# Recall of the fourth chunk placed in the first two steps of the feed-forward loop, with later feature splits and fewer, larger feature loads

## The chip, the core and the metric

The program runs on one core of a Trainium2 chip. A core has five engines with queues of their own: TensorE (PE) multiplies matrices into PSUM, VectorE (DVE), ScalarE (ACT) and GpSimd (POOL) work on vectors, and SyncE (SP) issues the transfers between memory and SBUF; sixteen DMA engines carry them. Each engine works through its own instructions in the order in which they stand; where an instruction waits on another engine, all that stands behind it on its queue waits too. The metric is the device time of one execution in microseconds (us), the median of some runs.

## The reference

`x` has 2048 tokens of 576 features. The result mixes an attention branch and a gated feed-forward branch by a gate that is computed for each token. The attention branch has 32 heads of 18 features and goes through the tokens in four chunks of 512; beside the attention inside a chunk, each chunk reads a memory that was summed over the chunks before it.

```python
scale = Dh ** -0.5
mask = (ar[:, None] < ar[None, :]) * (-1e9)
g = _sigmoid(beta).reshape(1, H, 1, 1)
for s in range(N):
    qs, ks, vs = q[:, :, s], k[:, :, s], v[:, :, s]
    p = _softmax(einsum("bhqd,bhkd->bhqk", qs, ks) * scale + mask)
    a_dot = einsum("bhqk,bhkd->bhqd", p, vs)
    pq = phi(qs)                                   # t + 1 where t > 0, else exp(t)
    num = einsum("bhld,bhde->bhle", pq, M)
    den = einsum("bhld,bhd->bhl", pq, z)[..., None] + 1e-6
    outs.append(g * num / den + (1.0 - g) * a_dot)
    pk = phi(ks)
    M = M + einsum("bhld,bhle->bhde", pk, vs)
    z = z + einsum("bhld->bhd", pk)
...
b = (_gelu(x @ w_gate) * (x @ w_up)) @ w_down
out = gate * (a @ wo) + (1 - gate) * b
```

## The kernel before

All large products are made from pairs of 16-bit words (a high and a low part), which ACT and POOL or DVE split off the 32-bit values. The program has two parts that matter here, and a last one (the output products) that doesn't.

**The projections** (lines 874 to 1171) go through the four chunks `s = 0..3` (the text counts them as chunks 1 to 4). In each, PE first makes the rows of `v` (`vrows`, eight products in four quarters `q`), and then nine products `j = 0..8` of 14 matmuls each (`project`, line 414), which give the columns of `q` and `k`. One product later `put_columns` takes such a product out of PSUM: ACT writes its high words (line 684) and, where features are needed, `relu` and `exp` (689, 690); DVE makes the positive part (697) and the low words (703); POOL adds the two into the feature tile `phi` (698). PSUM banks go round by name: `j = 0` has `dn`, 3 and 7 have `U`, 4 and 8 have `G`, the others `st` (two of them).

**The features of `q`** (`j` up to 4) of chunks 2 to 4 are needed with the features in rows. `split_phi` (658) makes words of each tile as soon as the next `put_columns` runs (ACT line 663, POOL line 664) and stores them to memory (`phq`, lines 666 and 667). `load_phi` (669) reads them back, a group of eight heads at a time: four pairs of heads, in two tiles of two pairs (three such tiles exist), by eight loads of 64 rows. `recall(s, g)` (751) multiplies a group by the memory (`mpair`), 16 small matmuls; `put_recall` (763) divides on DVE (771 to 775) and stores the result `mo` (two buffers) to `oms` (778). The recalls of chunks 2 and 3 stand in the quarters of the next chunk's rows; those of chunk 4 behind its products 6, 7 and 8 and behind the last `put_columns`.

**The memory.** `key_rows` and `memorize` sum the memory in PSUM, `keep_memory` (811, at `j = 1`) takes it out on DVE, and `memory_pairs` (826, at `j = 2`) squares it on ACT (829), sums the squares on PE (96), scales it on POOL, makes words of it and sends it through memory into `mpair` (851).

**Beside the products** `next_x` (945) squares the next chunk's input on ACT (159), sums the squares on POOL (166), lets PE sum over the rows (178), and makes words of the input with ACT (201) and DVE (218, 223). In chunk 4 the first weights of the feed-forward part are prepared instead: high words on ACT (343, 354), low words on POOL (347, 355), sums of blocks on POOL (332 to 337, `sums_g`).

**The feed-forward loop** (1855) runs 72 steps of `step(v)` (1497). A step is a fixed row of products (line 535, six matmuls of 128x512 each, and 1372) on the banks `G`, `V` and `U`, with DVE copies between them (1548, 1600, 1602, 1638), `gelu` on ACT (1367) and the split of the hidden words on ACT (1356) and POOL (1364). From step 4 on the attention inside the chunks is worked off beside it. Its tiles lie in the pools `keep` and `atn`, which are opened where the pool `prj` of the projections is closed.

The order of PE, ACT, DVE and POOL is that in which the code is written. The order of the transfers on SP isn't written by hand: a scheduler puts them there. Eight transfers can be under way before the next one waits for the oldest.

## Time and profile before

| | |
|---|---|
| time, median of 3 runs | 1616.96 us (1616.36 to 1617.0) |
| time of the profiled execution | 1616.14 us |
| its span, first to last instruction | 1614.1 us |
| PE busy | 1557.5 us |
| ACT, DVE, POOL busy | 1217.8, 1262.4, 1164.0 us |
| granted PE clock, mean | 0.986 |

The span is what the views of the profile cover; it is 2.0 us shorter than the time of its execution. In the views a row of the timeline gives the start, the duration, the line and the operation, with `xN` where N instructions in a row are merged, and in brackets the idle time of the engine ahead of it and what ended it. A row of the windows gives the busy time of each engine in a stretch, the granted clock of PE, the share of the DMA engines and what they moved. The rows themselves stand in the prediction.

### The profile page before, as it was taken

The page shows a single profiled execution, that of the slowest core. Times are in us where ns is not written, and L with a number is a line of the kernel's source. Part 1 is how long each engine was busy: PE and PEld are TensorE (multiplying, and loading weights), DVE is VectorE, ACT ScalarE, POOL GpSimd, SP SyncE. Part 2 cuts the span into 40 slices and gives each one's busy share as a digit, 9 for nine tenths or more (in the row PEclk, how much of TensorE's full clock was granted, in tenths as well). Part 3 has the DMA queues.
Part 4 walks back from the last instruction along what each step waited for, and adds up shares of the span by engine and source line. Part 5 has one row for each costly group of instructions (what it writes and reads, how often), then busy time and mean ns, then how long its engine had stood idle before and what let it go on. Part 6 is the DMA issues. An engine that isn't in the chain of part 4 may idle for free.

```text
span 1614.1 us, 34082 instructions
## 1 busy us (share of the span) xinstructions
PE 1557.5 (96%) x12271; PEld 944.9 (59%) x12271; DVE 1262.4 (78%) x3245; ACT 1217.8 (75%) x2092; POOL 1164.0 (72%) x1264
## 2 busy tenths in 40 slices
PE   9987867999999999999999999999999999999999
PEld 5644533456565665566565665666565665566577
DVE  7756764687888888888888888888888888888665
ACT  7565562487888888887889888888888888887421
POOL 5274481767778786867778786867878786867597
PEclk9999987999999999999999999999999999999999
DMA  6655665056575656666566767666575767755546
GB/s 242 224 154 177 207 179 151 31 102 131 121 141 118 145 139 143 139 132 133 121 145 116 154 129 154 143 131 136 118 151 117 154 137 148 138 122 105 111 84 174
DMA packets 514309, 225.85 MB, mean 140 GB/s; under 512 B 436920, under 2 KB 492956, under 8 KB 513628
## 3 DMA queue, kind: packets, MB, share of 16 engines
q1 hardware_dynamic: 514140, 223.68, 60.7%
q8 instruction: 96, 1.57, 0.4%
q14 instruction: 73, 0.60, 0.1%
HBM read 97.47 MB, written 37.52 MB: 84 GB/s over the span
## 4 chain that ended last, share of the span: by engine, by line
PE 82%; POOL 6%; ACT 3%; DVE 3%; DMA 3%; SPq 2%; issue 2%; POOLq 0%; ACTq 0%; DVEq 0%
PE dn L1326 25%; PE U L535 17%; PE G L535 11%; PE V L535 6%; PE V L1446 5%; PE pv L1279 4%; PE U L1372 2%; SPq L677 1%; PE V L1377 1%; PE G L1377 1%; PE st L1241 1%; PE V L1372 1%; PE G L1372 1%; POOL phi L698 1%; PE dn L421 1%
## 5 line engine op out<-in xcount | busy, mean ns | idle before, releaser
L535 PEld LDWEIGHTS <-pairg 128*128 128x128 f16 x2592 | 248.2, 98 | 262.5 <-issue 17.1
L1262 POOL TENSOR_TENSOR pl<-pb,ph 128x896 f16<-128x896 f32 (+1 forms) x128 | 185.3, 1469 | 210.5 <-ACT ph L1261 210.5
L1326 PE MATMUL dn<-paird,hhr 128*128 128x288 f16 x2115 | 328.7, 286 | 0.1
L1260 ACT ACTIVATE pb<-pb,mb,esc 128x512 f32<-128x512 f32 (+3 forms) x512 | 304.9, 642 | 5.5 <-POOL pl L1262 0.4
L1334 DVE SCALAR_TENSOR_TENSOR acc<-dn,ev,acc 128x288 f32<-128x288 f32 x533 | 262.6, 513 | 39.0 <-PE dn L1326 33.0
L1326 PEld LDWEIGHTS <-hhr 128*128 128x128 f16 x2160 | 207.0, 98 | 78.6 <-issue 11.8
L535 PE MATMUL G<-x,pairg 128*128 128x512 f16 x864 | 211.2, 381 | 2.6 <-DVE stage L703 2.4
L535 PE MATMUL U<-xt,pairg 128*128 128x512 f16 x864 | 210.3, 379 | 0.0
L1326 PE MATMUL dn<-paird,hhd 128*128 128x288 f16 x1275 | 209.9, 286 | 0.0
L1262 POOL TENSOR_TENSOR pb<-pb,ph 128x896 f16<-128x896 f32 (+1 forms) x128 | 179.6, 1403 | 33.8 <-ACT ph L1261 27.8
L1261 ACT ACTIVATE ph<-pb 128x896 f16<-128x896 f32 (+1 forms) x256 | 188.6, 737 | 9.7
L347 POOL TENSOR_TENSOR pairg<-raw,pairg 128x384 f16<-128x384 f32 (+2 forms) x144 | 156.6, 1109 | 16.7 <-ACT pairg L343 16.7
L1244 DVE CUSTOM_DVE_ANT_0 pb<-st,mask 128x512 f32<-128x512 f32 (+1 forms) x256 | 157.2, 614 | 0.0
L1326 PEld LDWEIGHTS <-hhd 128*128 128x128 f16 x1296 | 123.9, 98 | 50.5 <-issue 6.5
L1244 DVE CUSTOM_DVE_ANT_0 pb<-dn,mask 128x256 f32<-128x256 f32 (+1 forms) x192 | 67.2, 375 | 64.1 <-PE dn L1241 62.4
L1367 ACT ACTIVATE gl<-gl,sc 128x512 f32<-128x512 f32 x110 | 75.8, 715 | 46.7 <-DVE gl L1602 24.2
L535 PE MATMUL V<-x,pairg 128*128 128x512 f16 x426 | 105.0, 383 | 0.9 <-DVE gl L554 0.8
L1446 PE MATMUL V<-xt,nest 128*128 128x256 f16 x714 | 105.5, 272 | 0.2 <-DVE hold L1462 0.2
L535 PE MATMUL U<-x,pairg 128*128 128x512 f16 x432 | 105.0, 379 | 0.0
L414 PEld LDWEIGHTS <-wp 128*128 128x128 f16 x504 | 49.5, 100 | 73.9 <-issue 19.5
L1279 PEld LDWEIGHTS <-pt 128*128 128x128 f16 x2560 | 80.8, 96 | 13.1 <-issue 8.4
L1364 POOL TENSOR_TENSOR hhr<-gl,hhr 128x512 f16<-128x512 f32 x64 | 79.7, 1251 | 10.7 <-ACT hhr L1356 10.6
(377 smaller groups left out, 3229.2 us busy)
## 6 DMA issues: line engine op xcount, KB each, us to landing
qkt<-qk SPq DMA_DIRECT2D x256, 108.0 KB
raw<-in_wgu_dram SPq DMA_DIRECT2D x36, 640.0 KB
rawd<-in_wd_dram SPq DMA_DIRECT2D x36, 288.0 KB
qk<-stage SPq DMA_DIRECT2D x32, 256.0 KB
phg<-phq SPq DMA_DIRECT2D x96, 64.0 KB
qk<-stage SPq DMA_DIRECT2D x40, 128.0 KB
vp<-vstage SPq DMA_DIRECT2D x16, 296.0 KB
vt<-vp SPq DMA_DIRECT2D x16, 296.0 KB
```

What stands on the lines that cost most here:

```text
L347: pool.tensor_tensor(spot(f, *p, 1), raw_g[f][:, p[0] : p[1]], spot(f, *p, 0), OP.subtract)
L535: pe.matmul(o, w[:, i, (a + k) * P : (a + k + 1) * P], x[:, b + k], start=start and k == 0 and i == 0 and b == h, stop=k == 1 and i == 1, ...
L1244: dve.tensor_tensor_reduce(scored(a, qi), out[qi], mask[:, L - (qi + 1) * P :], 1.0, -3e38, OP.add, OP.max, mx[a][:, qi : qi + 1])
L1260: act.activation(r, r, AF.Exp, bias=b[:, qi : qi + 1], scale=esc[:, 0, c : c + 1])
L1261: act.activation(h[:, cols], p, AF.Copy)
L1262: pool.tensor_tensor(low[:, cols], p, h[:, cols], OP.subtract)
L1279: pe.matmul(ov, pr[:, 10 * i + COL[qi] // P + kb], v[:, 4 * e + kb, c0 : c0 + VC], start=kb == 0 and i == 0, stop=kb == qi and i == 1)
L1326: pe.matmul(o[:, :NH], hh[:, a, q * P : (q + 1) * P], w[:, b, n * NH : (n + 1) * NH], start=i == 0, stop=i == 5)
L1334: dve.scalar_tensor_tensor(av, o[:, :NH], ev, av, OP.mult, OP.add)
L1364: pool.tensor_tensor(hh[:, 1], t, hh[:, 0], OP.subtract)
L1367: act.activation(t, o, AF.Gelu_apprx_tanh, scale=scl[f // 2][0][:, 2 + c : 3 + c])
L1446: pe.matmul(o, w[:, (7 * c + i) * P : (7 * c + i + 1) * P], x[d], start=start and n == 0, stop=n == 2, skip_group_check=True)
```

## The change

The recalls of chunk 4 leave the projections: `recall(3, 0)` to `recall(3, 3)` now run inside steps 0 and 1 of the feed-forward loop, two in each, behind the product on `U` (line 1592 of before) and behind `product(Y, f, S4, ...)`. The pool `prj` therefore stays open until step 2, and `keep` and `atn` are opened there. `split_phi` takes a tile only four products after its own (two in chunk 4). `memory_pairs` is cut in two: the squares on ACT at `j = 1`, the rest at `j = 3` instead of 2. A group is loaded by two transfers of four pairs each into one tile of four pairs (two such tiles), and the first load of chunks 2 and 3 moves from `j = 6` to `j = 8`. `mo` has one buffer instead of two. `key_scale` moves from the product at which the next input is scaled into the first quarter of that chunk's rows, and its last operation from POOL to DVE. Every matmul of before is still there.

```diff
-            for i in range(2):
-                t = phg[s, g, i] = pp.tile([P, 2, L], F16, name="phg", bufs=3)
-                for e in range(2):
-                    for k in range(2):
-                        o = (8 * g + 4 * i + 2 * k + e) * n
-                        sp.dma_start(t[64 * e : 64 * e + 64, k], r[o : o + 64])
+            t = phg[s, g] = pp.tile([P, 4, L], F16, name="phg", bufs=2)
+            for e in range(2):
+                o = (8 * g + e) * n
+                sp.dma_start(t[64 * e : 64 * e + 64], r[o : o + 8 * n].rearrange("(k x) t -> x k t", x=2 * n)[:64])
...
-        def split_phi():
-            while phis:
+        def split_phi(until):
+            while phis and phis[0][:2] <= until:
...
-            split_phi()
+            split_phi((s, j - (2 if s == 3 else 4)))
...
-            mo = pp.tile([P, 4, 8 * DH], F32, name="mo", bufs=2)
+            mo = pp.tile([P, 4, 8 * DH], F32, name="mo", bufs=1)
...
-        def memory_pairs(s):
+        def memory_squares():
             q = pp.tile([P, 2], F32, name="msq", bufs=1)
             for i, c in enumerate((slice(0, DH), slice(DH, MC))):
                 act.activation(m16[:, :, 2, c], mc[:, :, c], AF.Square, accum_out=q[:, i : i + 1])
+            return q
+
+        def memory_pairs(s, q):
...
-            pool.tensor_scalar(ali[:, s], al[:, s, 0:3:2], iv, None, OP.mult)
+            dve.tensor_scalar(ali[:, s], al[:, s, 0:3:2], iv, None, OP.mult)
...
-                    key_scale(c)
...
+                        if q == 0:
+                            key_scale(s)
...
-                    if s and j == 2:
-                        memory_pairs(p)
+                    if s and j == 1:
+                        square = memory_squares()
+                    if s and j == 3:
+                        memory_pairs(p, square)
...
-                    if s and j == 6:
+                    if s in (1, 2) and j == 8:
                         load_phi(s, 0)
-                    if s == 3 and j > 5:
-                        recall(3, j - 6, (("V",), ("pv",)) if j == 7 else (("dn", 2), ("dn", 2)))
-                        load_phi(3, j - 5)
             put_columns(*done)
             finish_later()
-            recall(3, 3)
+            load_phi(3, 0)
             ahead[0] = first_product(0)
...
+            if v < 2:
+                recall(3, 2 * v)
+                load_phi(3, 2 * v + 1)
+                finish_later()
             product(X, f, A12, x1, 2, 6)
...
             product(Y, f, S4, x2_, 2, 6)
+            if v < 2:
+                recall(3, 2 * v + 1)
+                if v == 0:
+                    load_phi(3, 2)
+                finish_later()
...
+                if v == 2:
+                    prj.close()
+                    kp = tail.enter_context(tc.tile_pool(name="keep", bufs=2, side="right", reuse_waits="tile"))
+                    home.update(d=kp)
+                    ap_ = atn.enter_context(tc.tile_pool(name="atn", bufs=2, side="right", reuse_waits="tile"))
                 step(v)
```

**SP at the end of chunk 3's products.** `phg` is a group's features on their way back (line 677), `phq` their store, `raw<-in_wgu` the first weights of the feed-forward part, `qk` the words of a product. Before:

```order
L667 DMA phq_67<-stage 64x512
L666 DMA phq_67<-stage 64x1024
L708 DMA qk<-stage 128x2x512
L709 DMA qk<-stage 128x512
L677 DMA phg<-phq_67 64x512 x3
L708 DMA qk<-stage 128x2x512
L709 DMA qk<-stage 128x512
L243 DMA raw<-in_wgu_dram 128x1280 x3
```

Now:

```order
L243 DMA raw<-in_wgu_dram 128x1280
L668 DMA phq_67<-stage 128x1024
L669 DMA phq_67<-stage 128x512
L243 DMA raw<-in_wgu_dram 128x1280 x2
L708 DMA qk<-stage 128x2x512
L709 DMA qk<-stage 128x512
L677 DMA phg<-phq_67 64x4x512 x2
L668 DMA phq_67<-stage 64x1024
```

The first group's loads stood ahead of the three weight loads and now stand behind all of them, and behind the stores of the features of `j = 3`.

**ACT in the first products of chunk 4**, from the taking out of `j = 0`. `m` is the memory's tile of words, `msq` its sums of squares, `hhr`, `pairg` and `xt` words for the feed-forward part. Before:

```order
L690 ACTIVATE expm<-expm,lnv 128x512
L354 ACTIVATE hhr_2643<-raw 128x256
L343 ACTIVATE pairg<-raw 128x384
L343 ACTIVATE pairg<-raw 128x512
L457 ACTIVATE xt_2642<-acc,xsc 128x1024
L684 ACTIVATE stage<-st,unq 128x512
L689 ACTIVATE expm<-st,nal 128x512
L690 ACTIVATE expm<-expm,lnv 128x512
L663 ACTIVATE stage<-phi 128x512
L829 ACTIVATE m_103,msq<-mc 128x5x18
L829 ACTIVATE m_103,msq<-mc 128x5
L840 ACTIVATE m_103<-mt 128x5x19
```

Now:

```order
L690 ACTIVATE expm<-expm,lnv 128x512
L828 ACTIVATE m_103,msq<-mc 128x5x18
L828 ACTIVATE m_103,msq<-mc 128x5
L354 ACTIVATE hhr_2590<-raw 128x256
L343 ACTIVATE pairg<-raw 128x384
L343 ACTIVATE pairg<-raw 128x512
L457 ACTIVATE xt_2589<-acc,xsc 128x1024
L684 ACTIVATE stage<-st,unq 128x512
L689 ACTIVATE expm<-st,nal 128x512
L690 ACTIVATE expm<-expm,lnv 128x512
L457 ACTIVATE xt_2589<-acc,xsc 128x512 x2
L684 ACTIVATE stage<-st,unq 128x512
```

The squares moved ahead of the words of the weights and of the taking out of `j = 1`; the copy of the scaled memory (840, now 842) moved four rows further back, behind the taking out of `j = 2` and the first split of features.

**DVE in step 0**, from the copy of the product on `U`; `den` and `mo` are `put_recall`. Before:

```order
L775 TENSOR_TENSOR mo<-st,rden 128x288 x2
L1600 COPY gl<-U 128x512
L1602 TENSOR_TENSOR gl<-V,gl 128x512
L270 TENSOR_REDUCE z<-dn 128x2
L271 TENSOR_SCALAR z<-x_81,z 128x4
L274 TENSOR_SCALAR v<-z 128x2
L275 TENSOR_SCALAR pb<-z 128x4
L276 TENSOR_SCALAR v<-v 128x2
L277 TENSOR_SCALAR pb<-pb 128x4
L1638 TENSOR_TENSOR gl<-U,gl 128x512
L1349 SCALAR_TENSOR_TENSOR gl<-G,sc,gl 128x512
L554 COPY gl<-V 128x512
```

Now:

```order
L277 TENSOR_SCALAR pb<-pb 128x4
L770 TENSOR_SCALAR den<-st,eps 128x16 x2
L771 RECIPROCAL rden<-den 128x32
L772 TENSOR_TENSOR rden<-rden,ghs 128x32
L774 TENSOR_TENSOR mo<-st,rden 128x288 x2
L1642 TENSOR_TENSOR gl<-U,gl 128x512
L1349 SCALAR_TENSOR_TENSOR gl<-G,sc,gl 128x512
L554 COPY gl<-V 128x512
L309 TENSOR_SCALAR raw<-raw,sc 128x1280
L770 TENSOR_SCALAR den<-st,eps 128x16 x2
```

Two of the divisions now stand between the copies of step 0 that free the banks, and step 1 has two more.

More of the change, by code (lines that the diff above doesn't have):

```diff
@@ L493, in last_sum @@
         dve.scalar_tensor_tensor(flat(x[:, 4:6]), r[2, 1], sc, flat(x[:, 0:2]), OP.mult, OP.subtract)
-    phq = [dram.tile([D + 4, 3, L], F16, name=f"phq{i}", bufs=1) for i in range(3)]
+    phq = [dram.tile([D + DH, 3, L], F16, name=f"phq{i}", bufs=1) for i in range(3)]
     md = dram.tile([D, 3, MC], F16, name="md", bufs=1)
@@ L557 @@
     first, stay = ExitStack(), ctx.enter_context(ExitStack())
-    with tc.tile_pool(name="prj", bufs=2, side="right", reuse_waits="tile") as pp:
+    prj = ExitStack()
+    if True:
+        pp = prj.enter_context(tc.tile_pool(name="prj", bufs=2, side="right", reuse_waits="tile"))
         al = pp.tile([P, 4, 3], F32, name="al", bufs=1)
@@ L749, in first_words, with recall @@
                           start=k == 0, stop=k == 4)
-        def recall(s, g, banks=(("st", 2), ("st", 2))):
-            o = [bank(*i) for i in banks]
-            for i in range(2):
-                t = phg.pop((s, g, i))
-                for q in range(4):
-                    for k in range(2):
-                        c = (q % 2) * 8 * MC + (2 * i + k) * 2 * MC
-                        pe.matmul(o[q // 2][:, c : c + 2 * MC], t[:, k, q * P : (q + 1) * P], mpair[:, 4 * g + 2 * i + k],
-                                  start=i == k == q % 2 == 0, stop=i == k == q % 2 == 1, skip_group_check=True)
+        def recall(s, g):
+            o = [bank("st", 2) for _ in range(2)]
+            t = phg.pop((s, g))
+            for q in range(4):
+                for k in range(4):
+                    c = (q % 2) * 8 * MC + k * 2 * MC
+                    pe.matmul(o[q // 2][:, c : c + 2 * MC], t[:, k, q * P : (q + 1) * P], mpair[:, 4 * g + k],
+                              start=k == q % 2 == 0, stop=k == 3 and q % 2 == 1, skip_group_check=True)
             later.append(lambda: put_recall(s, g, o))
@@ L893 @@
             for r in phq:
-                sp.dma_start(r[D:].rearrange("f a t -> (f a) t"), mask.bitcast(F16)[:12])
+                sp.dma_start(r[D : D + 4].rearrange("f a t -> (f a) t"), mask.bitcast(F16)[:12])
             bdm = pa.tile([P, KT, 7 * MC], BF16, name="bdm", bufs=1)
@@ L1179, in scale_result @@
         scale_of(3, zo[:, 0:1])
-    with tc.tile_pool(name="keep", bufs=2, side="right", reuse_waits="tile") as kp, ExitStack() as tail:
-        home.update(d=kp)
+    with ExitStack() as tail:
         turns.update(of=2)
@@ L1187 @@
         atn = ExitStack()
-        ap_ = atn.enter_context(tc.tile_pool(name="atn", bufs=2, side="right", reuse_waits="tile"))
         UNITS = 4 * H
```

## The prediction

> **What bounds the kernel now.** I read the page first, then PE's waits and its timeline, then the queues that release it.
>
> ```profile
> PE 1557.5 (96%) x12271; PEld 944.9 (59%) x12271; DVE 1262.4 (78%) x3245; ACT 1217.8 (75%) x2092; POOL 1164.0 (72%) x1264
> PEclk9999987999999999999999999999999999999999
> ```
>
> PE is the bound; it idles 1614.1 - 1557.5 = 56.6 us, and the clock row shows where: slices 3 to 7 (of 40 us) alone are below 9, so nearly all that can be won lies in the products and rows of chunks 2 to 4 and the first step behind them. The windows and PE's timeline, for the end of chunk 4's products:
>
> ```profile
> 229.70:245.20 15.50, 1.02 (x16) 0.72 (x17) 4.50 (x7) 6.08 (x13) 11.63 (x12) 0.57 0.60 184
> 245.20:265.00 19.80, 12.82 (x88) 5.68 (x85) 9.05 (x23) 6.02 (x11) 2.66 (x3) 0.76 0.53 158
> 277.10:287.90 10.80, 10.80 (x51) 4.90 (x50) 7.83 (x17) 2.64 (x4) 8.65 (x12) 1.00 0.07 16
> ...
> 223.47 6.21 PE L414 MATMUL st<-x,wp 128*128 128x512 f16 x28
> 241.96 0.21 PE L759 MATMUL dn<-mpair,phg 128*128 128x38 f16 x1 [12.28 <-DMA phg<-phq]
> ...
> 245.22 4.99 PE L414 MATMUL U<-x,wp 128*128 128x512 f16 x14
> ...
> 260.60 1.87 PE L535 MATMUL G<-x,pairg 128*128 128x512 f16 x4 [2.44 <-DVE stage L703]
> ...
> 273.69 1.46 PE L535 MATMUL G<-x,pairg 128*128 128x512 f16 x6
> ```
>
> Columns of a window: length, then busy time of PE, its weight loads, DVE, ACT and POOL, granted clock, DMA share, GB/s. From 229.7 to 273.7 PE gets through two projections (6.2 us), four recalls (1.4) and 26 step matmuls (0.22 each by the row at 273.69: 5.6), 13 us of work, in 44 us: it waits for `phg`, and after each wait runs at half clock (14 matmuls in 4.99 against 6.21 / 2 = 3.1 us). SP is why the loads are late:
>
> ```profile
> 239.61 8.83 SPq L677 DMA_DIRECT2D phg<-phq  x14
> ...
> 257.92 5.13 SPq L677 DMA_DIRECT2D phg<-phq  x8
> 262.45 2.32 DMA phg<-phq
> ```
>
> A group takes eight issues of 0.6 us, and 2.3 us pass from the last issue to its landing. Earlier, the same path and the norms:
>
> ```profile
> 94.91 0.38 PE L178 MATMUL dn<-pairg,onesb 128*128 128x512 bf16 x1 [2.78 <-POOL pairg L166]
> ...
> 112.84 0.42 PE L423 MATMUL dn<-wv,x 128*128 128x288 f16 x1 [1.96 <-DVE x L223]
> ...
> 116.25 0.56 PE L759 MATMUL st<-mpair,phg 128*128 128x38 f16 x16
> ...
> 149.19 0.16 PE L96 MATMUL dn<-msq,onesb 128*128 128x2 bf16 x1 [1.15 <-ACT m L829]
> ...
> 160.37 0.59 PE L178 MATMUL V<-pairg,onesb 128*128 128x512 bf16 x1 [4.95 <-POOL pairg L166]
> ...
> 180.25 0.56 PE L759 MATMUL st<-mpair,phg 128*128 128x38 f16 x16
> ...
> 186.64 0.17 PE L96 MATMUL dn<-stat,onesb 128*128 128x10 bf16 x1 [3.45 <-ACT nest L91]
> ...
> PE st L759 <- DMA phg<-phq: 3.5, 4, 1.5
> PE st L759 <- DMA phg<-phq: 1.3, 2, 0.9
> ```
>
> The last two are the recalls in the rows, from 120 to 160 and from 160 to 200.
>
> **The change part by part.** All times below are on the clock of before. Prices, each from a row (those of ACT by the distance from one start to the next: taking out with features 0.6 + 0.7 + 0.6 = 1.9 us, a feature split 0.55):
>
> ```profile
> 226.04 0.67 ACT L684 ACTIVATE stage<-U,unq 128x512 f16<-128x512 f32 x1
> 226.61 0.68 ACT L689 ACTIVATE expm<-U,nal 128x512 f32<-128x512 f32 x1
> 227.31 0.72 ACT L690 ACTIVATE expm<-expm,lnv 128x512 f32<-128x512 f32 x1
> ...
> 213.07 0.93 DVE L824 TENSOR_TENSOR mc<-mc,mt 128x95 f32<-128x95 f32 x1
> ...
> 230.43 1.27 POOL L698 TENSOR_TENSOR phi<-phi,expm 128x512 f32<-128x512 f32 x1
> ...
> 232.44 1.15 POOL L664 TENSOR_TENSOR stage<-phi,stage 128x512 f16<-128x512 f32 x1 [0.74 <-DVE stat L87]
> ...
> 237.24 2.26 POOL L347 TENSOR_TENSOR pairg<-raw,pairg 128x640 f16<-128x640 f32 x2
> 239.58 0.72 POOL L332 TENSOR_TENSOR raw<-raw 128x256 f32<-128x256 f32 x1
> ...
> 242.66 0.45 POOL L337 TENSOR_TENSOR raw<-raw 128x128 f32<-128x128 f32 x1
> ```
>
> *Chunk 4's end.* The wait for the memory's squares goes (1.1 us, as at 149.19), so the last three projections end at about 235.4 and the first product at 236.7. What is late next is bank `G`, which the first product of step 0 needs and `j = 8` holds. ACT must take it out, and stands in its queue behind words of weights that wait for POOL's sums (332 to 337). In order: the squares now wait for `mc` (214.0, ahead of two weight words and `j = 1`); taking out `j = 1` ends at 218.8, `j = 2` at 222.0, the memory's scaling on POOL at 224.7, `j = 3` at 228.3, `j = 4` at 230.6; three splits, `j = 5` and the next weight words, 233.2; POOL's two low words 237.0 and its five sums 240.6; ACT's words 241.6, two squares, `j = 8` 243.9, DVE's low words 244.5. With 1 us for POOL operations that DVE slows, PE starts step 0 at 245.5. From there to the product that before started at 273.69 are 20 step matmuls (4.3), a recall (0.36, as in 257.83's seven in 0.33) and 1.8 us of slow clock: 252.0. **Gain 21.7.** The load of the first group issues behind DVE's low words, lands about 250 and is wanted at 251.6, so PE doesn't see it.
>
> Steps 0 and 1 pay for it: three more recalls on PE (1.1 us) and four divisions on DVE:
>
> ```profile
> 268.42 0.37 DVE L771 TENSOR_SCALAR den<-st,eps 128x16 f32<-128x16 f32 x2
> 268.83 0.35 DVE L772 RECIPROCAL rden<-den 128x32 f32<-128x32 f32 x1
> 269.21 0.19 DVE L773 TENSOR_TENSOR rden<-rden,ghs 128x32 f32<-128x32 f32 x1
> 269.44 0.82 DVE L775 TENSOR_TENSOR mo<-st,rden 128x288 f32<-128x288 f32 x2
> ```
>
> That is 1.75 us each, two a step: 7.83 + 3.5 = 11.3 of a step of 10.8 + 0.7 = 11.5 us. DVE just keeps up; queued behind each division are the copies that free `U`, `G` and `V`. I take 0.8 us. **Net 19.8**; bounds 14 (each division delays PE by its length) and 23 (no slow clock).
>
> *Chunk 2's products and the rows after.* ACT's memory squares wait for `mc` and end at 79.8; then come `j = 1` (81.8), three squares of the next input (83.3) and `j = 2` (85.3). There ACT waits until POOL has scaled the memory, 88.1, because the squares are summed on PE only behind `j = 3` (85.9); words 88.7, two more squares 89.7. POOL sums these (166) with no feature split ahead of them: 92.3 instead of 94.9, and the input's scale is known at 94.1. `key_scale` with its wait of DVE for POOL is gone from here; four operations of 0.15 us on DVE in the rows replace it, beside PE's products. ACT's three words of the input end at 95.3, 98.7 and 101.6, one behind each of `j = 4` to 6 and a split, DVE's last (223) at 103 instead of 112.8, so PE, at full clock, reaches the recall at 105.1 instead of 116.25. But the splits are late now: POOL's words of `j = 3`, behind ACT's taking out of `j = 7`, end at 105.5; SP issues the stores, two `qk` and only then the two loads (107 to 108). What 256 KB take from issue to landing no row shows; the bounds are 2.3 us (64 KB, above) and 5.9 us (640 KB, below). I take 3.5, nearer the first. The Trainium skill ("DMA: Bandwidth & Descriptors", Anatomy of one DMA) fits 2.0 us plus bytes at 436 GB/s for the GpSimd path, an estimate of 2.6 us here, which would give 0.9 us more at this recall. PE waits until 111, then runs slow for 1.5 us. In the rows, the 3.5 us of `phg` waits go, but DVE is the next bound:
>
> ```profile
> 130.10:136.40 6.30, 5.64 (x71) 4.79 (x68) 6.11 (x13) 2.65 (x5) 2.43 (x2) 1.00 0.59 179
> ```
>
> 6.11 of 6.30 us are DVE's, so a quarter can't drop far below 6.1. **Gain 3.7 at the keys, 0.8 in the rows: 4.5**; bounds 1 and 9.
>
> *Chunk 3's products.* The squares' wait goes (1.15). The norm's doesn't: ACT has the memory's squares at 145.4, words of a sum 146.4, `j = 1` 148.3, three squares 149.9, `j = 2` 151.8, waits for POOL until 154.6, words 155.2, two squares 156.3; DVE and POOL add them by 158.1 instead of 160.4, and PE, done with `j = 4` at 154.1, waits four of its five us. ACT's words of the input then end at 161.6, 165.8 and 169.1, ahead of PE, which reaches the rows at 172.0 and the recall at 175.5. Its loads stand behind the weights:
>
> ```profile
> 177.95 1.41 SPq L243 DMA_DIRECT2D raw<-in_wgu_dram  x3
> ...
> 178.44 5.86 DMA raw<-in_wgu_dram
> ```
>
> SP issues the last two weight loads at 174 (behind POOL's 172.6), `phg` at 176. If the transfers are served in turn, 1.9 MB in 6.3 us by these rows, `phg` lands at 181.8, later than before's 180.25; if not, at 179.5. I take 181.8. The statistics' wait (186.64) is then already over, so the next recall comes at 188.2 instead of 190.9. **Gain 2.7**; bounds 0 and 5. The Trainium skill ("DMA: Bandwidth & Descriptors", Queues, rings and completion order) says that on each DMA engine descriptors are consumed in ring order: by that rule 181.8, without it 179.5 and 2.3 us more gain. No row of before shows a small load issued right behind a large one.
>
> *Rows of chunk 4:* waits of 1.3 us go and, from 200 on, a like sum of small ones; DVE lets 0.7 through. *Operations that two engines slow by sharing:* -2, by rows like POOL's 2.29 for an addition of 1.27:
>
> ```profile
> 191.40:198.30 6.90, 5.63 (x71) 4.76 (x67) 6.80 (x15) 1.71 (x5) 1.07 (x2) 1.00 0.52 156
> ...
> 226.28 2.29 POOL L698 TENSOR_TENSOR phi<-phi,expm 128x512 f32<-128x512 f32 x1
> ```
>
> *Pools that open at step 2:* the attention's first loads now stand on SP behind the last store of `mo`, early in step 2; they are used in step 4, two steps of 10.8 us later, which hides them. Without that cover a load would cost its landing, 2.3 to 5.9 us, once.
>
> Sum: 19.8 + 4.5 + 2.7 + 0.7 - 2 = 25.7 us. The profiled execution's 1616.1 us (0.8 below the median) becomes 1590.4; the steps after 2 are unchanged.
>
> **Rivals.** *The loads of chunks 2 and 3 land in time* (256 KB in 2.3 us, out of turn behind the weights): +1.2 and +2.3, with the rows' 3.5 in full +2: 1584.9. For it speaks that eight issues become two. *The waits come back in the recalls and the steps* (landing 5.9 us; DVE late by each division; ACT late at `G` by 3 more): -2.4 - 6.2 - 3 = -11.6: 1602.0. Against it DVE's 7.83 in a step.
>
> *Slower:* `mo` has one buffer, so DVE's division waits until the last store of `mo` has landed; all of DVE's copies stand behind it. A store takes about 2.3 us by the row of a load, and the next `mo` is written 6.3 - 0.7 = 5.6 us later, so nothing is lost. If SP, held by loads that wait for a recall, let the store land 10 us after, each of the eight recalls in rows would lose 4.4 us, 35 in all: 1625.6. It decides from 25.7 / 8 = 3.2 us each, a landing after 8.8 us. Against it: the order puts each store ahead of loads that wait longer than it.
>
> *The edit does nothing:* the order shows the recalls in the steps, so only if `G` frees PE as late as before: then 1616.
>
> **How the numbers follow.** Forecast (1586 to 1597) 0.55; loads in time 0.17; waits come back 0.20; nothing 0.04; slower 0.04. The range from 1582 to 1603 leaves out 0.2. A measurement of this kernel tells 0.2%, 3.2 us, from no change: faster 0.92, same 0.04, slower 0.04.
>
> **What would show it.** Right: the 12.28 us wait gone, a wait of 7 to 10 us of the first product on `G` for DVE or ACT; waits of 4 to 6 us at the first recalls of chunks 2 and 3 for `phg`; granted clock near 1 from 250 on; two divisions a step in DVE with steps 0 and 1 under 12.5 us. Wrong: PE waiting for `phg` in step 0, a store of `mo` ending DVE's waits, or step 4 waiting for tiles of the pools that open later.

## The result, and the profile after

| | before | changed |
|---|---|---|
| time, median (us) | 1616.72 (1616.36 to 1617.0) | 1596.62 (1595.5 to 1597.24) |
| profiled execution: time, span (us) | 1616.14, 1614.1 | 1595.5, 1593.3 |
| granted PE clock, mean | 0.986 | 0.989 |

The changed kernel takes 0.9875 of the time of before (95% interval 0.9858 to 0.9892): 20.1 us less. The forecast's sum was 25.7 us less, and its 1590.4 us lie 26.3 below this median of before. The page of the changed kernel, its busy times and its clock row:

```profile
PE 1548.6 (97%) x12271; PEld 942.6 (59%) x12271; DVE 1264.1 (79%) x3249; ACT 1218.2 (76%) x2092; POOL 1161.5 (73%) x1260
PEclk9999898999999999999999999999999999999999
```

PE has the same 12271 matmuls, 8.9 us less busy time (fewer of them run while the granted clock is low) and 44.7 us idle instead of 56.6: 20.8 in all, the difference of the spans. Of the clock row two slices are below 9 as before, 8 and 8 for 8 and 7 (the forecast's "slices 3 to 7" misread that row; no term rests on it). PE's timeline of the changed kernel, the rows that answer to those of before:

```profile
72.24 3.19 PE L414 MATMUL dn<-x,wp 128*128 128x512 f16 x14
...
91.93 0.38 PE L178 MATMUL dn<-pairg,onesb 128*128 128x512 bf16 x1 [0.52 <-POOL pairg L166]
...
114.91 0.67 PE L758 MATMUL st<-mpair,phg 128*128 128x38 f16 x16 [7.98 <-DMA phq<-stage]
...
135.28 3.18 PE L414 MATMUL dn<-x,wp 128*128 128x512 f16 x14
...
155.39 0.38 PE L178 MATMUL V<-pairg,onesb 128*128 128x512 bf16 x1 [3.96 <-POOL pairg L166]
...
183.99 0.67 PE L758 MATMUL st<-mpair,phg 128*128 128x38 f16 x16 [11.00 <-DMA phg<-phq]
...
191.23 0.56 PE L758 MATMUL st<-mpair,phg 128*128 128x38 f16 x16
...
203.89 3.18 PE L414 MATMUL dn<-x,wp 128*128 128x512 f16 x14
...
243.78 2.72 PE L535 MATMUL G<-x,pairg 128*128 128x512 f16 x6 [9.46 <-DVE stage L703]
...
250.57 1.46 PE L535 MATMUL G<-x,pairg 128*128 128x512 f16 x6
...
277.08 1.46 PE L549 MATMUL pv<-xt,hhr 128*128 128x512 f16 x6
```

The wait of 12.28 us for `phg` at the end of chunk 4's products is gone and one of 9.46 on bank `G` stands there; the norms come 3 and 5 us sooner (94.91 and 160.37 before; 2.5 and 2.3 us counted from each chunk's `j = 0`); and two new waits, 7.98 and 11.00 us, stand at the first recalls of chunks 2 and 3. The row of the first of them names a store, which SP issued at 111.21, right behind the two loads of the group that the recall reads (109.81). The starts in the timeline of before that the prediction doesn't show:

```profile
72.74 3.19 PE L414 MATMUL dn<-x,wp 128*128 128x512 f16 x14
...
137.96 3.18 PE L414 MATMUL dn<-x,wp 128*128 128x512 f16 x14
...
206.22 3.19 PE L414 MATMUL dn<-x,wp 128*128 128x512 f16 x14
...
298.72 1.46 PE L549 MATMUL pv<-xt,hhr 128*128 128x512 f16 x6
```

The same starts in both timelines, and the gain of each section between them:

| PE reaches | before | changed | gain in the section |
|---|---|---|---|
| chunk 2's `j = 0` | 72.74 | 72.24 | 0.5 |
| chunk 3's `j = 0` | 137.96 | 135.28 | 2.2 |
| second recall of chunk 3 | 190.91 | 191.23 | -3.0 |
| chunk 4's `j = 0` | 206.22 | 203.89 | 2.6 |
| product on `G` in step 0 (273.69 before) | 273.69 | 250.57 | 20.8 |
| fourth product of line 549, the one for step 3 | 298.72 | 277.08 | -1.5 |
| end of the span | 1614.1 | 1593.3 | -0.8 |

So the whole gain is in the stretch from chunk 4's `j = 0` to the first products of step 0. In chunks 2 and 3 what the norms gave is taken back by the first recalls. SP's timeline of the changed kernel shows the second of them (start, time of the issues, number merged):

```profile
171.11 0.46 SPq L243 DMA_DIRECT2D raw<-in_wgu_dram  x1
...
172.59 1.00 SPq L243 DMA_DIRECT2D raw<-in_wgu_dram  x2
...
175.12 1.39 SPq L677 DMA_DIRECT2D phg<-phq  x2
```

and its windows, where the last two columns are the share of the DMA engines and GB/s:

```profile
172.00:176.00 4.00, 0.98 (x8) 0.54 (x6) 2.12 (x7) 2.73 (x6) 2.29 (x3) 1.00 0.96 289
176.00:180.00 4.00, 0.00 (x0) 0.00 (x0) 0.00 (x0) 2.26 (x7) 3.42 (x4) 0.53 1.00 372
180.00:184.00 4.00, 0.01 (x1) 0.04 (x2) 0.58 (x2) 1.07 (x4) 0.00 (x0) 0.50 1.11 310
```

The loads are issued by 176.5 and PE starts at 183.99, 7.5 us later. All that time the DMA engines are full: 3.9 MB pass from 172 to 184 (4 us each of 289, 372 and 310 GB/s), of which the three weight loads of 640 KB are at most 2.0 and the group 0.5; the other 1.4 MB are mostly stores of words and features.

ACT's timeline of the changed kernel shows why `G` is late, ahead of step 0:

```profile
239.54 1.04 ACT L343 ACTIVATE pairg<-raw 128x384 f16<-128x384 f32 x2 [1.20 <-POOL raw L337]
...
242.02 0.58 ACT L684 ACTIVATE stage<-G 128x512 f16<-128x512 f32 x1
```

The taking out of `j = 8` (242.02) stands behind words of weights that wait for POOL's sums, as the forecast had it. But that wait is only 1.20 of the 9.46 us. The rest is work that stands ahead in ACT's queue, and two waits of 1.82 and 1.02 us (at 231.19 and 234.36) in which ACT needs a `stage` buffer that a store of features still holds.

### The profile page after: what moved, and what is told of

Same layout as the page of the kernel before. It is cut to its first block, busy times and chain, and to the rows that moved or that the text cites. A ratio compares the mean times of both kernels' runs of the same rounds, so it can differ in the third digit from the quotient of the medians.

```text
span 1593.3 us, 33961 instructions
## 1 busy us (share of the span) xinstructions
PE 1548.6 (97%) x12271; PEld 942.6 (59%) x12271; DVE 1264.1 (79%) x3249; ACT 1218.2 (76%) x2092; POOL 1161.5 (73%) x1260
## 4 chain that ended last, share of the span: by engine, by line
PE 81%; POOL 6%; DVE 4%; ACT 3%; DMA 3%; issue 1%; SPq 0%; POOLq 0%; ACTq 0%; DVEq 0%
PE dn L1326 25%; PE U L535 17%; PE G L535 11%; PE V L535 6%; PE V L1446 5%; PE pv L1279 4%; PE U L1372 2%; PE G L1377 1%; PE V L1377 1%; PE st L1241 1%; PE V L1372 1%; PE G L1372 1%; POOL pairg L1787 1%; PE dn L1241 1%; PE st L414 1%
## 5 line engine op out<-in xcount | busy, mean ns | idle before, releaser
L1334 DVE SCALAR_TENSOR_TENSOR acc<-dn,ev,acc 128x288 f32<-128x288 f32 x533 | 262.7, 513 | 39.3 <-PE dn L1326 33.3
L1326 PEld LDWEIGHTS <-hhr 128*128 128x128 f16 x2160 | 207.0, 98 | 78.9 <-issue 12.1
L1279 PEld LDWEIGHTS <-pt 128*128 128x128 f16 x2560 | 80.8, 96 | 13.1 <-issue 8.4
```

Of the source, the lines that this page charges most:

```text
L1279: pe.matmul(ov, pr[:, 10 * i + COL[qi] // P + kb], v[:, 4 * e + kb, c0 : c0 + VC], start=kb == 0 and i == 0, stop=kb == qi and i == 1)
L1326: pe.matmul(o[:, :NH], hh[:, a, q * P : (q + 1) * P], w[:, b, n * NH : (n + 1) * NH], start=i == 0, stop=i == 5)
L1334: dve.scalar_tensor_tensor(av, o[:, :NH], ev, av, OP.mult, OP.add)
```

## The experiments

Each kernel was compared with the kernel before on its own chip, which ran that at 1614.1 (e1 to e4), 1617.0 (e5 to e8) or 1614.3 us (e9 to e12). So the ratios are compared, not the times; the last column is the difference from 0.9875 in 1616.7 us. Intervals of 0.0017 and 0.0015 make one of about 3.7 us for such a difference. The timelines tell more: the stretch from chunk 2's `j = 0` to chunk 4's, and that from there to the fourth product of line 549 (277.08 above). Where a kernel left a stretch as in the changed kernel, the first came out at 131.7 to 132.6 us (e1, e4, e5) and the second at 73.2 to 73.6 (e2, e3, e11); the first of e3, e9 and e12, which are alike there, is up to 2 us apart.

| kernel | time | ratio, 95% interval | stretches | against the changed kernel |
|---|---|---|---|---|
| before | 1616.7 | 1 | 133.5, 92.5 | +20.2 |
| changed | 1596.6 | 0.9875 [0.9858, 0.9892] | 131.7, 73.2 | |
| e1 recalls of chunk 4 back | 1607.8 | 0.9956 [0.9941, 0.9971] | 132.1, 85.3 | +13.1 |
| e2 early splits | 1594.3 | 0.9872 [0.9858, 0.9887] | 130.4, 73.2 | -0.5 |
| e3 first loads sooner | 1592.6 | 0.9860 [0.9843, 0.9877] | 128.1, 73.6 | -2.4 |
| e4 taking out of `j = 8` first | 1598.3 | 0.9898 [0.9883, 0.9912] | 132.2, 74.7 | +3.7 |
| e5 the same, chunk 4's loads sooner | 1592.7 | 0.9856 [0.9842, 0.9871] | 132.6, 69.0 | -3.1 |
| e6 small loads | 1603.6 | 0.9921 [0.9902, 0.9939] | 140.4, 73.2 | +7.4 |
| e7 first loads soonest, and e5 | 1590.6 | 0.9839 [0.9818, 0.9861] | 132.1, 68.4 | -5.8 |
| e8 e7 and another bank | 1589.6 | 0.9835 [0.9820, 0.9849] | 131.0, 67.3 | -6.5 |
| e9 e3 and e8's end of chunk 4 | 1586.4 | 0.9824 [0.9807, 0.9840] | 129.2, 67.6 | -8.2 |
| e10 norm's part back | 1596.0 | 0.9880 [0.9865, 0.9895] | 132.4, 73.0 | +0.8 |
| e11 `key_scale` back | 1597.4 | 0.9891 [0.9876, 0.9905] | 133.4, 73.2 | +2.6 |
| e12 e9, squares later | 1585.1 | 0.9816 [0.9801, 0.9831] | 127.2, 67.0 | -9.5 |

**e1: chunk 4's recalls back in its products**, with its splits one product later and its first load at `j = 6` as before; the loads stay of four pairs.

```diff
-            split_phi((s, j - (2 if s == 3 else 4)))
+            split_phi((s, j - (0 if s == 3 else 4)))
...
+                    if s == 3 and j == 6:
+                        load_phi(3, 0)
+                    if s == 3 and j > 5:
+                        recall(3, j - 6, (("V",), ("pv",)) if j == 7 else (("dn", 2), ("dn", 2)))
+                        load_phi(3, j - 5)
             put_columns(*done)
             finish_later()
-            load_phi(3, 0)
+            recall(3, 3)
```

> Chunk 4's four recalls stand again behind its products 6, 7, 8 and the last taking out, its features are split one product later and its first group is loaded at j = 6; the loads of four pairs, the late splits of chunks 2 and 3, the norm and the rest of the change stay. Theory 1 (the place of the recalls made the gain at chunk 4's end: PE's queue stands behind each wait for features): the time rises to 1609 to 1617, PE waits 8 to 14 us for phg at the recalls between 225 and 250, and step 0 starts at 255 to 261 instead of 243.8. Rival (the number of issues made it: eight issues of 0.6 us a group, 8.83 us for 14 of them): with two issues a group the waits are under 4 us in sum and the time stays at 1597 to 1602.

PE's timeline of e1, then SP's:

```profile
244.08 0.69 PE L758 MATMUL dn<-mpair,phg 128*128 128x38 f16 x16 [16.49 <-DMA phg<-phq]
244.60 4.96 PE L414 MATMUL U<-x,wp 128*128 128x512 f16 x14
```

```profile
227.66 0.59 SPq L677 DMA_DIRECT2D phg<-phq  x1
...
240.10 1.95 SPq L677 DMA_DIRECT2D phg<-phq  x3
```

Theory 1 held in its place and, nearly, in its size (1607.8 for 1609 to 1617): PE waits 16.49 us with two products still to do, and 14 matmuls then take 4.96 us. The rival fell. But the reason isn't only where PE's queue stands: the scheduler put the second load of the first group 12.4 us behind the first on SP, between stores, so how much a better place of that one load would give back stays open. Of the change's 20.2 us, 13.1 come with the place of the recalls and of what feeds them (12.1 by the second stretch). The other 7.2 us of that stretch (85.3 for 92.5 before) e1 keeps; which of the other parts brings them no run tells.

**e6: the old form of the loads**, eight of 64 rows for a group, at the changed kernel's places.

```diff
-            t = phg[s, g] = pp.tile([P, 4, L], F16, name="phg", bufs=2)
-            for e in range(2):
-                o = (8 * g + e) * n
-                sp.dma_start(t[64 * e : 64 * e + 64], r[o : o + 8 * n].rearrange("(k x) t -> x k t", x=2 * n)[:64])
+            for i in range(2):
+                t = phg[s, g, i] = pp.tile([P, 2, L], F16, name="phg", bufs=3)
+                for e in range(2):
+                    for k in range(2):
+                        o = (8 * g + 4 * i + 2 * k + e) * n
+                        sp.dma_start(t[64 * e : 64 * e + 64, k], r[o : o + 64])
```

> Only the form of the loads is undone: a group is again eight loads of 64 rows into tiles of two pairs, at the changed kernel's places. Theory 1 (eight issues of 0.6 us hold SP 3.5 us longer than two of 0.65): the first recalls of chunks 2 and 3 wait 1 to 3 us longer, the rows and steps 0 and 1 get waits for phg of 2 to 8 us in sum back, time 1600 to 1608. Rival (the number of issues is hidden behind the products): 1596 to 1599.

SP's timeline of e6, then PE's at the first two groups of chunk 2:

```profile
117.24 4.94 SPq L679 DMA_DIRECT2D phg<-phq  x8
```

```profile
112.92 0.55 PE L761 MATMUL st<-mpair,phg 128*128 128x38 f16 x8 [4.27 <-DMA phg<-phq]
...
123.26 0.18 PE L761 MATMUL st<-mpair,phg 128*128 128x38 f16 x1 [1.44 <-DMA phg<-phq]
```

Theory 1 held in the time, 7.4 us, and in its place only in part: the first recall of chunk 3 waits 2.3 us more than in the changed kernel, as it said, but that of chunk 2 waits 2 us less (6.0 for 7.98). The loss is all in the first stretch (140.4 for 131.7), most of it in the rows: the later recalls there wait up to twice for single loads of their group, 0.6 us apart as SP issues them. The second stretch is the same as with large loads: in the steps their form is hidden. That the place of the recalls and the form of the loads make 13.1 + 7.4 = 20.5 us, nearly the 20.2 of the change, is chance and no account of it. The change gains 19.3 of its 20.2 us in the second stretch (92.5 to 73.2), and e6 has all of these with small loads; in the first it gains 1.8 (133.5 to 131.7), where the small loads cost 8.7.

**e2: the features split at once**, the first group loaded at `j = 6`.

```diff
-            split_phi((s, j - (2 if s == 3 else 4)))
+            split_phi((s, j - (2 if s == 3 else 0)))
...
-                    if s in (1, 2) and j == 8:
+                    if s in (1, 2) and j == 6:
                         load_phi(s, 0)
```

> In chunks 2 and 3 the features are split at the next taking out again and the first group is loaded at j = 6; loads of four pairs, norm, and chunk 4 as in the changed kernel. Theory 1 (the late splits make the first recalls wait, 7.98 and 11.00 us): both waits fall under 2 us; but POOL has the splits ahead of the sums of squares again, so the norms come at 94 to 95 and 157 to 160 instead of 91.9 and 155.4, and the time is 1590 to 1597. Rival (DVE bounds the rows, whatever the recall does): the waits go, chunk 3's j = 0 still starts at 135 to 136.5 and chunk 4's at 203 to 205, and the time is within 2 us of the changed kernel or slower by what the norms lose.

PE's timeline of e2:

```profile
94.34 0.38 PE L178 MATMUL dn<-pairg,onesb 128*128 128x512 bf16 x1 [2.64 <-POOL pairg L166]
...
115.77 0.68 PE L758 MATMUL st<-mpair,phg 128*128 128x38 f16 x16
...
158.88 0.59 PE L178 MATMUL V<-pairg,onesb 128*128 128x512 bf16 x1 [7.59 <-POOL pairg L166]
...
178.48 0.56 PE L758 MATMUL st<-mpair,phg 128*128 128x38 f16 x16
```

Both waits for features are gone, and the norms are late again; the time is that of the changed kernel. The first recall of chunk 2 comes at 115.77, of the changed kernel at 114.91. So with the loads where the change puts them the late splits bring nothing that can be measured: PE waits for features instead of the norm and the words of the input. Both theories gave such numbers; e3 tells them apart. With early splits the first stretch is 3.1 us shorter than before (130.4 for 133.5), with all of the change's other parts there, so nothing shows the form of the loads to be worth 7.4 us there.

**e10: the memory's squares and sums together at `j = 2` again**, the splits late.

```diff
-                    if s and j == 1:
-                        square = memory_squares()
-                    if s and j == 3:
-                        memory_pairs(p, square)
+                    if s and j == 2:
+                        memory_pairs(p, memory_squares())
```

> Only the move of the memory's squares and sums is undone: squares on ACT, their sum on PE and the scaling on POOL stand together at j = 2 again. Theory 1 (as predicted: the squares' wait on PE and the place of POOL's scaling delayed the norms): PE waits about 1.1 us for msq in chunks 3 and 4 again, the norms come 1 to 3 us later than 91.9 and 155.4; but in chunks 2 and 3 the first recall waits for features behind them anyway, so of this the time shows 1 to 3 us: 1597.5 to 1600. Rival (the late splits alone had freed the norms): norms within 0.5 us, time 1596 to 1597.5.

PE's timeline of e10:

```profile
92.68 0.38 PE L178 MATMUL dn<-pairg,onesb 128*128 128x512 bf16 x1 [0.74 <-POOL pairg L166]
...
148.00 0.17 PE L96 MATMUL dn<-msq,onesb 128*128 128x2 bf16 x1
...
157.21 0.38 PE L178 MATMUL V<-pairg,onesb 128*128 128x512 bf16 x1 [2.98 <-POOL pairg L166]
```

The rival held in the main. By the clock of the span the norms are 0.75 and 1.8 us later than in the changed kernel, which is more than the rival's 0.5, but the chunks start later too. The wait for the squares (1.15 at 149.19 before) doesn't come back, and from each chunk's `j = 0` to its norm it takes 19.9 and 19.1 us, in the changed kernel 19.7 and 20.1. With e2 (squares moved, splits early: 21.8 and 23.7) this settles it: the late splits free the norms, and the move of the squares brings nothing that can be seen here. That e2 loads at `j = 6` isn't the reason: e7 below does so with late splits, and takes 19.7 and 20.1.

**e11: `key_scale` beside the products again**, its last operation on POOL.

```diff
-                        if q == 0:
-                            key_scale(s)
...
                     for i in range(3):
                         outscale(c, i)
+                    key_scale(c)
...
-            dve.tensor_scalar(ali[:, s], al[:, s, 0:3:2], iv, None, OP.mult)
+            pool.tensor_scalar(ali[:, s], al[:, s, 0:3:2], iv, None, OP.mult)
```

> Only key_scale is undone: it stands beside the products again, where the next input is scaled, with its last operation on POOL. Theory 1 (as predicted: DVE's wait for POOL there held the words of the input, PE's wait for the last of them at 112.8 before): PE waits 3 to 8 us for words of the input at the first rows of chunks 2 and 3 instead of 1.95, but the first recall, which waits 7.98 and 11.00 us behind it, takes this up: time 1596 to 1598. Rival (it delays what recall(1,0) waits for as well): 1599 to 1603.

Half of theory 1 fell: PE's wait for the last word of the input is 2.00 us (1.95 in the changed kernel, 1.94 to 3.17 in the other kernels here with `key_scale` as changed), not 3 to 8. The time lies where theory 1 had it, but it (2.6 us more, interval 3.7) and the first stretch (133.4 for 131.7 to 132.6) are both too near to those of the changed kernel to tell; whether this part brings anything stays open.

**e3: the first loads one product sooner**, the splits late.

```diff
-                    if s in (1, 2) and j == 8:
+                    if s in (1, 2) and j == 7:
                         load_phi(s, 0)
```

> Only the first load of chunks 2 and 3 stands one product sooner (j = 7 for 8), so that on SP it is ahead of the stores of the features of j = 2 or 3 and, in chunk 3, ahead of all three weight loads; the splits stay as late as in the changed kernel. Theory 1 (the wait is SP's order and the transfers ahead in turn, not the splits themselves): recall(2,0) waits under 3 us instead of 11.00, recall(1,0) under 4 instead of 7.98, time 1587 to 1592. Rival (256 KB loads take 4 to 8 us wherever they stand, or DVE bounds the rows behind): the wait moves to the next recalls or to the key rows, time 1594 to 1597.

SP's timeline of e3 in chunk 3, then PE's:

```profile
171.09 1.27 SPq L677 DMA_DIRECT2D phg<-phq  x2
...
173.54 1.50 SPq L243 DMA_DIRECT2D raw<-in_wgu_dram  x3
```

```profile
113.22 0.67 PE L758 MATMUL st<-mpair,phg 128*128 128x38 f16 x16 [4.88 <-DMA phg<-phq]
...
176.03 0.67 PE L758 MATMUL st<-mpair,phg 128*128 128x38 f16 x16 [4.53 <-issue]
183.76 0.17 PE L96 MATMUL dn<-stat,onesb 128*128 128x10 bf16 x1 [2.59 <-ACT nest L91]
```

Issued by 172.4, ahead of the weights, the same 512 KB let PE start at 176.03, 3.7 us later instead of 7.5. This is the place's price, shown by one edit. The Trainium skill ("DMA: Bandwidth & Descriptors", Queues, rings and completion order) has descriptors consumed in ring order on each DMA engine; these two runs agree with it, with 3.7 us ahead of the weights and 7.5 behind them. The Trainium skill's fit for the GpSimd path ("DMA: Bandwidth & Descriptors", Anatomy of one DMA), 2.6 us as an estimate in the forecast, is below the 3.7 of this row, where SP issued the loads and the DMA engines were full (share 1.00 from 172 to 176). The waits are above the bounds that theory 1 gave (3 and 4 us), and part of the gain goes to the statistics' wait behind (2.59). The first stretch falls by 3.6 us, so DVE wasn't yet the bound of the rows; the time, 2.4 us less with an interval of 3.7, wouldn't show that alone.

**e7: the first loads at `j = 6`** (`if s in (1, 2) and j == 6`), and e5 (below).

> e5, and the first loads of chunks 2 and 3 at j = 6 (two products sooner than in the changed kernel, one sooner than in e3), the splits as late as in the changed kernel. Theory 1 (the waits at the first recalls are SP's order): recall(1,0) and recall(2,0) wait 1.5 to 3.5 us each (4.88 and 4.53 in e3), chunk 4's j = 0 starts 4 to 6 us sooner than the changed kernel's 203.9, and with e5's gain the time is 1586 to 1589. Rival (DVE bounds the rows): chunk 4's j = 0 at 200 to 201 as in e3, time 1588 to 1591.

PE's timeline of e7, then ACT's:

```profile
112.30 0.56 PE L758 MATMUL st<-mpair,phg 128*128 128x38 f16 x16 [1.99 <-DMA phg<-phq]
...
122.11 0.69 PE L758 MATMUL st<-mpair,phg 128*128 128x38 f16 x16 [3.81 <-DMA phg<-phq]
```

```profile
112.93 0.63 ACT L665 ACTIVATE stage<-phi 64x512 f16<-64x512 f32 x1 [3.62 <-DMA phq<-stage]
```

The first recalls wait 1.99 and 1.89 us, as theory 1 said, and it helps nothing: the first stretch is 132.1. The loads now stand ahead of the stores of features, so ACT waits 3.62 us for a `stage` buffer (0.99 at this place in e3, 1.06 in e5), the last split comes late, and with it the second group, for which PE waits 3.81; the statistics' wait of chunk 3's rows grows to 5.42. Neither theory had this: between too late and too soon the product before the last is the best of the three places tried.

**e4: the taking out of chunk 4's `j = 8` ahead of the weight words.**

```diff
+                    if (s, j) == (3, 8):
+                        put_columns(*done)
                     beside_products(s, j)
...
-            put_columns(*done)
-            finish_later()
             load_phi(3, 0)
```

> At j = 8 of chunk 4 the taking out of that product stands on ACT, DVE and POOL ahead of the weight words and squares of that place instead of behind them. Theory 1 (G is held because ACT's taking out of j = 8 stands behind words that wait for POOL's sums): PE's wait for G falls from 9.46 to 4 to 6 us, ACT's wait for POOL's sums stays but holds nobody, and the time falls by 3 to 5 us to 1591.5 to 1594. Rival (the first product of step 0 waits for DVE's order or the steps behind wait for the words that now come later): the time stays within 1.5 us of 1596.6.

PE's timeline of e4, then SP's:

```profile
240.29 2.72 PE L535 MATMUL G<-x,pairg 128*128 128x512 f16 x6 [4.84 <-DVE stage L703]
...
251.07 0.55 PE L758 MATMUL st<-mpair,phg 128*128 128x38 f16 x16 [3.88 <-DMA phg<-phq]
```

```profile
241.76 0.47 SPq L668 DMA_DIRECT2D phq<-stage  x1
...
246.17 6.06 SPq L677 DMA_DIRECT2D phg<-phq  x5
```

The wait on `G` fell by 4.6 to 4.84 us as theory 1 said, so ACT's order at `j = 8` makes half of it; the other half is what ACT is behind when it gets there (DVE, which frees the bank, waits 4.15 us for ACT one product earlier). But the stretch became longer (74.7 for 73.2): the recall of step 0 now waits 3.88 us for loads that SP issues behind the stores of the last split (POOL does that behind its sums). The wait was theory 1's, the time neither theory's. The forecast had noted that these loads land at about 250 and are wanted at 251.6: with `G` sooner that cover was gone.

**e5: e4, with chunk 4's first two groups loaded at `j = 6`.**

```diff
+                    if s == 3 and j == 6:
+                        load_phi(3, 0)
+                        load_phi(3, 1)
-            load_phi(3, 0)
...
-                load_phi(3, 2 * v + 1)
+                if v == 0:
+                    load_phi(3, 2)
...
-                    load_phi(3, 2)
+                    load_phi(3, 3)
```

> As e4 (the taking out of chunk 4's j = 8 ahead of the weight words), and the first two groups of chunk 4 are loaded at j = 6, ahead of the stores that wait for POOL's split of the last tile; the later two behind the two recalls of step 0. Theory 1 (in e4 the freed 4.6 us at G were lost again to the 3.88 us wait for phg behind SP's stores and to the slow clock after it): no recall of steps 0 and 1 waits for phg over 0.5 us, G waits 4 to 5.5 us, and from chunk 4's j = 0 to the second first_product (254.02 - 203.89 = 50.1 us in the changed kernel) it takes 45 to 46.5; time 1591 to 1593. Rival (DVE's copies and divisions bound step 0): the stretch stays at 49 to 50 and the time at 1596 to 1597.

No recall of the steps waits for `phg`, `G` waits 4.87, and from chunk 4's `j = 0` to the second product of line 549 it takes 45.9 us for 50.1. Theory 1 held.

**e8: e7, and bank `dn` for chunk 4's `j = 8`.**

```diff
-                pr = bank("dn", 2) if s and j == 0 or i == 4 else bank("G") if i == 0 else bank("U") if i == 3 else bank("st", 2)
+                pr = bank("dn", 2) if s and j == 0 or i == 4 else bank("dn", 2) if (s, j) == (3, 8) else bank("G") if i == 0 else bank("U") if i == 3 else bank("st", 2)
```

> e7, and chunk 4's j = 8 uses a bank dn instead of G, so that the first product of step 0 has a free G. Theory 1 (G is only the first of two holds: the next product needs V, which DVE frees behind its words of j = 8): the wait for G goes, a wait of 4 to 5 us on V for DVE's copy (line 554) takes its place, and the time falls by 0 to 2 us below e7's. Rival (the bank alone was the hold): no wait over 1 us between the products of chunk 4 and step 0, and 4 to 5 us less than e7.

PE's timeline of e8:

```profile
239.29 2.72 PE L535 MATMUL V<-x,pairg 128*128 128x512 f16 x6 [3.89 <-DVE gl L554]
```

`G` isn't waited for any more, and `V` is, as theory 1 said: the second stretch falls by 1.1 us.

**e9: e3 and e8's end of chunk 4.**

> The changed kernel with e3's first loads (j = 7 in chunks 2 and 3) and e8's end of chunk 4 (taking out of j = 8 ahead of the weight words, bank dn for j = 8, first two groups loaded at j = 6). If the gains stand in separate places and add: from chunk 2's j = 0 to chunk 4's j = 0 e3 took 128.07 us against 131.65 of the changed kernel, from there to first_product(3) e8 took 67.29 against 73.19, together 9.5 us less: 1586 to 1588.5. Rival (the loads of chunk 4 or the clock give part back): 1589 to 1592.

The two gains add, mostly: stretches of 129.2 and 67.6 us, 1586.4 us.

**e12: e9, two squares on ACT behind the taking out of `j = 8`.**

```diff
-                    if j == 7:
-                        squares(1, 3, 0, act_square)
-                        squares(1, 0, 2, act_square)
                     if j == 8:
                         first_pairs(1)
                         high_g(1, 1)
                         low_g(1, 1)
+                        squares(1, 3, 0, act_square)
+                        squares(1, 0, 2, act_square)
```

> e9, and the two squares on ACT of chunk 4's j = 7 (0.9 us each with the read of the sum) stand behind the taking out of j = 8 too. Theory 1 (ACT's queue ahead of the taking out of j = 8 sets when step 0 runs): PE's wait on V for DVE's copy falls by 1.5 to 1.8 us from 3.9, and the time by about that below e9's: 1584.5 to 1587. Rival (ACT then waits for a stage buffer or POOL, or the statistics of the weights come too late for step 1): within 0.7 us of e9.

ACT's timeline of e12:

```profile
230.21 0.63 ACT L665 ACTIVATE stage<-phi 64x512 f16<-64x512 f32 x1 [1.61 <-DMA phq<-stage]
...
233.04 0.60 ACT L684 ACTIVATE stage<-dn 128x512 f16<-128x512 f32 x1 [0.64 <-DMA phq<-stage]
```

The 1.8 us of squares went and longer waits for `stage` buffers (1.61 and 0.64 us, for 1.22 here in e9) took more than half of their place; the second stretch falls by 0.6 us. By the stretch the rival held. e12 is the fastest kernel measured: 0.9816 of before, 9.5 us (with an interval of about 3.7) below the changed kernel.

## Why the prediction was right, and where its sizes were off

The time, 1596.6 us, lies in the range and on the side that was forecast; it is 6.2 us above the forecast. The main step, at chunk 4's end, came as it was worked out. That the sum is no further off is in part luck: the two sections with the first recalls brought 8.0 us less than forecast, and the rows of chunk 4 and the 2 us that were taken off for sharing gave 3.9 back. By its steps:

- **Chunk 4's end** (gain 21.7): 20.8. The step came as worked out: the next wait is on `G`, behind ACT's queue, and 9.46 us long, where 7 to 10 was the sign of being right; counted from chunk 4's `j = 0` step 0 was to start after 39.3 us (245.5 - 206.22) and did after 39.9. e4 shows that ACT's order at `j = 8` is half of that wait, and e1 that without the move PE waits for features.
- **Steps 0 and 1** (-1.9): -1.5. Four divisions fit beside DVE's copies.
- **Chunk 2's products and the rows after** (4.5): 2.2. The norm came at 91.93 and PE reached the recall at 106.9 for 105.1. The step that was off is the issue of the loads, 109.8 to 111.1 instead of 107 to 108. About half of that is POOL's splits: two of them took 2.1 and 1.6 us instead of 1.15. The 3.5 us of landing were 3.8. The wait of 7.98 us is longer than the 4 to 6 that were named as a sign.
- **Chunk 3's products to the second recall** (2.7): -3.0. This is the mis-sized term, 5.7 us. That the transfers go in turn behind the weights was right. Counted from chunk 3's `j = 0`, SP began to issue the loads after 39.8 us instead of 38.0 (176 - 137.96), and PE started 8.9 us after that instead of 5.8: the sum had the weights' 1.9 MB alone ahead, and not the stores that fill the engines too. Together that is 4.9 us; the last 0.8 lies between the first recall and the second, which are 7.2 us apart instead of 6.4. The statistics' wait is gone, as the forecast had it, but the wait for features in its place is longer, 11.00 us, where 4 to 6 were named as a sign. Where the weights stand behind (e3) it is 3.7 us from the last issue instead of 7.5.
- **Rows of chunk 4** (0.7) gave 2.6; **sharing** (-2) isn't seen as a term of its own; some of it is in the late issue of chunk 2's loads.
- **The reason given for the norms was wrong in part.** The forecast followed both the memory's squares and the splits through ACT and POOL. By e10 and e2 the splits alone free the norms, and by e2 their gain and the waits that they cause cancel, where the forecast had 7.2 us of gain from chunk 2's `j = 0` to the second recall of chunk 3 (4.5 and 2.7).
- **The loads' form** was costed at 1.5 us in the rows, because DVE bounds a quarter. Against the kernel before that may be: e2, with early splits, is 3.1 us shorter in the first stretch with all of the other parts. With late splits e6 shows it worth 7.4 us: it is what makes late splits bearable.

Of the rivals, *waits come back* is the one that partly came, at the first recalls, and not in the steps: there PE waits for no features, and the granted clock is 1.00 from 250 on. Two divisions a step fit: from the second product of line 549 to the third and the fourth it takes 11.8 and 11.3 us, below the 12.5 of the forecast's sign. *`mo` with one buffer* wasn't tried by itself, but its mechanism, DVE waiting for a store of `mo`, shows in DVE's timeline of the changed kernel once, with 0.23 us of the 4.4 that it needed at each recall:

```profile
123.24 0.82 DVE L774 TENSOR_TENSOR mo<-st,rden 128x288 f32<-128x288 f32 x2 [0.23 <-DMA om<-mo]
```

## What to carry to other kernels

An instruction that waits for a transfer holds up everything that stands behind it in its engine's queue (16.49 us in e1): put it where that engine has other work, and look at once for what is late next, since here each wait removed uncovered another, smaller one (12.28 us for features, then 9.46 and 4.84 on bank `G`, 3.89 on bank `V`). Work put off to free one engine moves a wait to whoever needs its result: before it is put off, move the load's issue ahead of large transfers that nobody needs yet, and price a load behind them by all bytes on their way ahead of it, stores included (7.5 us here for the 3.7 without the weights ahead). A load can also stand too soon: ahead of stores whose buffers an engine needs it stops that engine (3.62 us of ACT in e7).

## What was not expected of the hardware

POOL and DVE hold each other up for some pairs of operations. POOL's timeline of the changed kernel, and DVE's at the same time:

```profile
159.74 1.26 POOL L698 TENSOR_TENSOR phi<-phi,expm 128x512 f32<-128x512 f32 x1
160.96 2.15 POOL L666 TENSOR_TENSOR stage<-phi,stage 128x512 f16<-128x512 f32 x1
...
170.43 1.15 POOL L666 TENSOR_TENSOR stage<-phi,stage 128x512 f16<-128x512 f32 x1
```

```profile
159.86 2.23 DVE L218 SCALAR_TENSOR_TENSOR x<-raw,xsc,x 128x1024 f16<-128x1024 f32 x1
```

The same split takes 1.15 us at 170.43 and 2.15 beside DVE's word of the input. By these rows the two take turns rather than share: DVE's operation ends at 162.09, 1.1 us after POOL's addition ahead of the split (161.00), and the split ends 1.0 us after DVE's (163.11). In e5 DVE began first in chunk 2: its operation took 1.28 us at 100.17, and POOL's addition at 100.24 took 2.34 instead of 1.26. That these two have something that only one can use at a time is an inference from such rows; no run was made for it. In the forecast this was a flat 2 us; it belongs at the splits, where in chunk 2 it delayed the loads.
